# Attention feeding a two-layer PReLU network: three reorderings where one batch element's second layer hands over to the next one's first layer

## The chip, the core and the metric

One NeuronCore of a Trainium2 chip runs the whole program. The metric is the device time of one execution in microseconds (us); lower is better. The profile shows one execution with every instruction of TensorE (PE, its weight loads as PEld), VectorE (DVE), ScalarE (ACT), GpSimd (POOL) and the issue queue of SyncE (SP, its rows are SPq).

## The reference

Four batch elements, eight heads, 768 positions, head width 64. Attention is restricted by hashing: a query sees only keys whose six sign bits under a random projection agree with its own. Its output, as 3072 tokens of width 512, goes through two layers with a PReLU between them:

```python
scores = np.where(q_bucket == k_bucket, scale * q @ k.T, -1e9)
attn = softmax(scores)                       # per batch element and head
x = (attn @ v).transpose(0, 2, 1, 3).reshape(3072, 512)
h = x @ w_in                                 # 512 x 2048
g = np.maximum(h, 0) + alpha * np.minimum(h, 0)
out = g @ w_out                              # 2048 x 512
```

All tensors are float32.

## The kernel before

The program has two stages. Until about 313 us it runs the attention for all 16 pairs of heads and prepares the weights. After that it runs the two layers for each batch element b from 0 to 3, 768 tokens at a time, as a list `blocks`: for each b eight blocks `"1"` (first layer, `ff1`) and seven blocks `"2"` (second layer, `ff2`). A fallback program behind a flag never runs with these inputs.

**Seven products instead of eight.** Each layer splits both operands in halves both ways, and forms the product of the 2 x 2 blocks from seven block products with sums of blocks (the scheme of Strassen, in Winograd's form). `Product` holds the steps of one block: step 1, 2, 5, 6, 3, 7, 4 are groups of matmuls into the PSUM tiles a, b and c, each followed by copies on ScalarE or additions on VectorE. Step 22 is only VectorE work: additions of what steps 1 and 2 made. Step 4 is the last one; its matmuls go into a, and the addition after it (`finish("21", ...)`, the row L1243 `m<-m,z_4a` where the block is the second layer's last) completes the block and frees the PSUM slot.

**Sums ahead of the products.** x's halves for element b are `x_0`, `x_1`, `x_2`, `x_5`; `sum_x(b, n, DVE)` (L891) makes the four derived operands `x_3` to `x_6`, one for each n. `x_6`, of n = 3, is read only by step 4 of a first-layer block.

**The nested unit.** For b = 1, 2 and 3 two of the seven first-layer products are themselves formed by seven products, for four blocks at a time. `unit(b, u, before)` does that for blocks 4u to 4u + 3, by two `Inner` objects, `one` (operand `x_0`) and `two` (operand `x_3`), whose steps it interleaves with the last step of the block before it, `before.step(4)`. Matmul rows of `one` write na, nb, nc, those of `two` nd, ne, nf (L1084). Tiles a, c and d come from a pool of three PSUM slots (`two_banks`), which z_4a uses as well: nd takes the slot of z_4a.

The nested products need sums of their own. `sum_inner_x(b, o)` (L1062 to L1064) makes three tensors `xn` out of x_0 (o = 0) or x_3 (o = 1); the first reader of the latter is nf. `sum_inner(b, u, o)` (L1051) makes four nested sums of w_in, tile `wn` for o = 0 and `wp` for o = 1; it works for b = 1 alone, and after each sum GpSimd stores it to memory (`w_n_s`, L1052), from where b = 2 and 3 load it. The first reader of `wn`'s sums is nc, that of `wp`'s is nf.

**Order.** `do` keeps the instructions of an engine in the order in which the program makes them; `pinned` does so only under a condition, and what is not pinned is placed by a scheduler. Every engine works through its own list in order: an instruction that waits holds up all behind it on that engine. The order of calls around the handover is written by hand. In the block that ends a batch element (`"2"`, n == 6) it is: step 22, steps 5 (begun earlier), 6 and 3, `sum_inner(b + 1, 0, 0)`, step 7, `sum_inner_x(b + 1, 1)`, `sum_x(b + 1, 3, DVE)`; then `unit` begins.

**Output.** `turn_out` transposes a finished quarter of the output on VectorE (L1271) into a tile `o` and stores it by twelve DMAs (L1278), each of 32 partitions with rows of 256 bytes. The quarters are named by p: 2 and 3 are stored in the second layer, 5 and 4 both at the end of the next `unit`. All are issued by SyncE, but for four of the last batch element. SyncE also issues nearly all loads, among them each first-layer block's weights (`load_w`, L897, tile `wi`, three buffers, so that block n + 3's load waits until block n is done).

Of the kernel before, what the change touches and what calls it, by code (L numbers as in the profile page):

```python
# [407 lines left out]
def fast_path(  # L408
# [12 lines left out]
    nc = tc.nc  # L421
    P = 128
    B, H, S, D = q.shape
# [20 lines left out]
    PE, DVE, ACT, POOL = nc.tensor, nc.vector, nc.scalar, nc.gpsimd  # L444
# [253 lines left out]
    def two_banks(name):  # L698
        return psum.tile([P, 2, 512], F32, name=name, tag="sc", bufs=3)
# [172 lines left out]
    def pinned(when, ins):  # L872

        if when:
            do(ins)
# [10 lines left out]
    def sum_x(b, n, engine):  # L886

        to, a, c = ((3, 5, 0), (5, 2, 5), (4, 2, 3), (6, 4, 1))[n]
        if to != 5:
            x_m[b, to] = mid.tile([P, 2, CW], F32, name=f"x{b}_{to}", tag=f"x{to}", bufs=1)  # L890
        do(engine.tensor_tensor(x_m[b, to], x_m[b, a], x_m[b, c], op=ALU.subtract))  # L891
# [154 lines left out]
    def sum_inner(b, u, o):  # L1046

        if b != 1:
            return
        for m, x, op, y in ((3, 21, ALU.add, 2), (4, 3, ALU.subtract, 0), (5, 0, ALU.subtract, 21), (6, 1, ALU.subtract, 4)):  # L1050
            do(DVE.tensor_tensor(n_w[b, u, o, m], n_w[b, u, o, x], n_w[b, u, o, y], op=op))  # L1051
            nc.gpsimd.dma_start(w_n_s[u, o, :, m - 3].rearrange("p (t f) -> p t f", t=2), n_w[b, u, o, m])  # L1052

    def sum_inner_x(b, o):

        x = x_m[b, 3 * o]
        if o == 0:
            t = mid.tile([P, 4, HC], F32, name=f"xn{b}_0", tag="x", bufs=1)
        else:
            t = late[0].tile([P, 4, HC], F32, name=f"xn{b}_1", tag="gs5", bufs=1)  # L1060
        left, right = (x[:, :, c * HC : (c + 1) * HC] for c in range(2))
        do(DVE.tensor_tensor(t[:, :2], right, x[:, 0].rearrange("p (c w) -> p c w", c=2), op=ALU.subtract))  # L1062
        do(DVE.tensor_tensor(t[:, 2], right[:, 1], t[:, 0], op=ALU.subtract))
        do(DVE.tensor_tensor(t[:, 3], left[:, 1], t[:, 2], op=ALU.subtract))  # L1064
        n_x[b, o] = {0: left[:, 0], 1: left[:, 1], 2: right[:, 1], 3: t[:, 0], 4: t[:, 2], 5: t[:, 1], 6: t[:, 3]}
# [68 lines left out]
    def unit(b, u, before):  # L1134

        def bank(name, tag=None):
            name = f"n{name}{b}_{u}"
            return psum_bc[0].tile([P, 512], F32, name=name, tag=tag) if tag else two_banks(name)[:, 0]

        one = Inner(b, u, 0, bank("a"), bank("b", "b"), bank("c"))  # L1140
        one.step(1)
        one.step(5)
        before.step(4)
        one.step(2)
        one.step(6)
        if not u:
            sum_inner(b, 0, 1)
        two = Inner(b, u, 1, bank("d"), bank("e", "b"), bank("f", "c"))
        two.step(1)
        one.step(3)  # L1150
        two.step(5)
        one.step(7)
        two.step(2)
        two.step(6)
        one.step(4)
        two.step(3)
        now = ff1(b, 4 * u)
        now.step(1)
        two.step(7)
        now.step(2)  # L1160
        now.step(5)
        two.step(4)
        if u:
            sum_w2(b, 0, 3, 4, 6, 5)
        turn_out()
        return now

# [35 lines left out]
    def sides_g(b, n):  # L1203
        t = g_m[b, SIDES[ORDER[n]][1]]
        for m, kh, ch in ((0, 0, 0), (1, 1, 0), (2, 1, 1), (12, 0, 1)):
            g2[b, n, m] = t[:, kh * HK : (kh + 1) * HK, ch * HC : (ch + 1) * HC]

    def sum_w2(b, n, *ms):

        if n < 7:  # L1210
            for m in ms:
                x, op, y = {
                    3: (21, ALU.add, 2), 4: (3, ALU.subtract, 0), 5: (0, ALU.subtract, 21), 6: (1, ALU.subtract, 4),
                }[m]
                w2[b, n, m] = t = late[0].tile([P, HK, H2], F32, name=f"ws{b}_{n}_{m}", tag=f"ws{m}", bufs=1 + (m < 5))
                do(DVE.tensor_tensor(t, w2[b, n, x], w2[b, n, y], op=op))  # L1216
# [49 lines left out]
    def turn_out():  # L1266
        while to_turn:
            b, p, half, ch = to_turn.pop(0)
            o = late[0].tile([P, CW, 2], F32, name=f"o{b}_{p}", tag="o")
            for i in range(2):  # L1270
                do(DVE.transpose(o[:, :, i], m2[b, p][:, i]))  # L1271

            src = o.rearrange("p (c w d) i -> p c w (d i)", c=CH, d=32)
            for a in range(DM // 128):
                for c in range(CH):
                    cols = slice(half * DM // 2 + 64 * a, half * DM // 2 + 64 * a + 64)
                    queue = nc.gpsimd if (b, p) == (B - 1, 3) and c % 2 else nc.sync
                    pinned(b + 1 < B, queue.dma_start(  # L1278
                        out_v[b, ch * CH + c].rearrange("(w r) d -> r w d", r=32)[:, :, cols],
                        src[32 * a : 32 * a + 32, c],  # L1280
                    ))
# [187 lines left out]
    for j, (b, what, n) in enumerate(blocks):  # L1469
        n2 = n + 1 if what == "2" else 0 if n == NI - 1 else 7  # L1470
        if n2 == 0:
            sides_g(b, 0)
            if b == 0:
                sum_w2(b, 0, 3, 4)
        if not j:
            now.step(6)
        elif not (b and what == "1"):
            now.step(2)
        if j == 0:
            now.step(3)  # L1480
            now.step(7)
            now.step(2)
        now.step(22)
        if (b, what, n) == (1, "2", 1):
            largest()
        if what == "2" and b + 1 < B and 2 <= n < 6:
            if n == 3:
                sum_inner_x(b + 1, 0)
            else:
                sum_x(b + 1, {2: 0, 4: 1, 5: 2}[n], DVE)  # L1490
        if b and what == "1" and n == 1:
            load_inner(b, 1)
        if b and what == "1" and n in (2, 3):
            sum_inner(b, 1, n - 2)
        if 0 < n2 < 7:
            sides_g(b, n2)
            sum_w2(b, n2, 3, 4)
        if n2 < 7:
            sum_g2(b, n2, 3, 4)
        if j:  # L1500
            if not (b and what == "1"):
                now.step(5)
            now.step(6)
            now.step(3)
            if n2 or b == 0:
                sum_w2(b, n2, 6)
            if what == "2" and n == 6 and b + 1 < B:
                sum_inner(b + 1, 0, 0)
            if b and what == "1" and (n + 1) % 4:
                after = ff1(b, n + 1)  # L1510
                after.step(1)
            now.step(7)
            if n2 or b == 0:
                sum_w2(b, n2, 5)
            sum_g2(b, n2, 5)
        if (b, what, n) == (1, "2", 3):
            verdict()

        for n_out in [(), (0,), (1,), (2, 3), (4,), (5, 6), (7,)][j] if j < 7 else ():
            sum_out(n_out)  # L1520
        for n_out in [(1,), (2, 3), (4,), (5, 6), (7,)][j] if j < 5 else ():
            load_out(n_out)
        if what == "1":
            load_w(b * NI + n + 3)

            if b and n in (2, 5):
                load_w2(b, n // 4)
            if not b and n >= NI - 2:
                load_w2(b, n - NI + 2)
        else:  # L1530
            load_w2(b, n + 2)
            if b + 1 < B:
                if n == 5:
                    load_inner(b + 1, 0)
                if n == 0:
                    load_x(b + 1)
                if n == 6:
                    sum_inner_x(b + 1, 1)
                    sum_x(b + 1, 3, DVE)
        if j + 1 == len(blocks):  # L1540
            turn_last(0)
        elif what == "1" or n < 6:
            turn_out()
        before = now
        if j + 1 < len(blocks):
            b1, what1, n1 = blocks[j + 1]
            if b1 and what1 == "1" and n1 % 4 == 0:
                now = unit(b1, n1 // 4, before)
            elif b1 and what1 == "1":
                now = after  # L1550
                now.step(2)
                now.step(5)
                before.step(4)
            else:
                now = ff1(b1, n1) if what1 == "1" else ff2(b1, n1)
                now.step(1)
                before.step(4)
        else:
            before.step(4)
        if n2 < 7:  # L1560
            sum_g2(b, n2, 6)
# [29 lines left out]
```

## Time and profile before

| | us |
|---|---|
| median of 3 runs | 866.96 (865.55 to 867.17) |
| the profiled execution | 867.4 |
| its span, first to last instruction | 865.6 |
| attention stage | 0 to 313 |
| first layer b = 0 | 313 to 385 |
| handover to b = 1, 2, 3 (first matmul `na`) | 449.60, 585.65, 720.47 |

The profile's busy table gives, for each engine, its busy time, the share of the span and the instructions. A row of a timeline has start, duration, engine, line, operation, output <- inputs, shapes and the number of merged instructions; in square brackets stands how long the engine sat idle before it and what released it. Matmuls are pipelined and their ends are modelled, so the distance between the starts of two groups says more than a duration does. A row of waits says which group of instructions waited for which, for how long in total, how many times and for how long at most.

### The profile page before, as it was taken

The page shows a single profiled execution, that of the slowest core. Times are in us where ns is not written, and L with a number is a line of the kernel's source. Part 1 is how long each engine was busy: PE and PEld are TensorE (multiplying, and loading weights), DVE is VectorE, ACT ScalarE, POOL GpSimd, SP SyncE. Part 2 cuts the span into 40 slices and gives each one's busy share as a digit, 9 for nine tenths or more (in the row PEclk, how much of TensorE's full clock was granted, in tenths as well). Part 3 has the DMA queues.
Part 4 walks back from the last instruction along what each step waited for, and adds up shares of the span by engine and source line. Part 5 has one row for each costly group of instructions (what it writes and reads, how often), then busy time and mean ns, then how long its engine had stood idle before and what let it go on. Part 6 is the DMA issues. An engine that isn't in the chain of part 4 may idle for free.

```text
span 865.6 us, 15105 instructions
## 1 busy us (share of the span) xinstructions
PE 853.1 (99%) x5602; PEld 590.5 (68%) x5602; DVE 751.6 (87%) x1210; ACT 415.7 (48%) x778; POOL 123.8 (14%) x265
## 2 busy tenths in 40 slices
PE   9999999999999999999999999999999999999996
PEld 4444444444444445569997769997668998577996
DVE  6999999999999977899995979996769997668986
ACT  7777888878788833331115541114452114353111
POOL 1322423333334310210000100000000000000001
PEclk9999999999999999999999999999999999999999
DMA  8966879879697436776342935343845434650242
GB/s 198 184 141 131 199 178 244 167 202 246 131 249 209 146 126 237 247 283 225 116 137 69 348 135 169 121 148 82 310 150 177 141 109 122 215 219 5 98 153 72
DMA packets 180036, 147.97 MB, mean 171 GB/s; under 512 B 126977, under 2 KB 161969, under 8 KB 176369
## 3 DMA queue, kind: packets, MB, share of 16 engines
q1 hardware_dynamic: 166688, 118.92, 47.1%
q0 software_dynamic: 10256, 26.66, 10.0%
q10 hardware_dynamic: 3008, 1.33, 0.6%
q8 instruction: 46, 0.75, 0.4%
q14 instruction: 38, 0.30, 0.1%
HBM read 115.35 MB, written 30.41 MB: 168 GB/s over the span
## 4 chain that ended last, share of the span: by engine, by line


## 5 line engine op out<-in xcount | busy, mean ns | idle before, releaser
L790 ACT ACTIVATE pt<-sc 128x768 f32<-128x768 f32 x192 | 153.9, 813 | 3.0 <-PE sc L787 2.8
L787 PE MATMUL sc<-qT,kT 64*128 64x384 f32 x768 | 155.3, 482 | 0.0
L820 PE MATMUL av<-pt,vn 128*32 128x385 f32 (+1 forms) x1536 | 127.0, 485 | 0.0
L820 PEld LDWEIGHTS av<-pt,vn 128*32 128x32 f32 x1536 | 50.3, 109 | 73.8 <-issue 69.2
L787 PEld LDWEIGHTS sc<-qT,kT 64*128 64x128 f32 x768 | 68.5, 187 | 37.6 <-issue 37.3
L983 DVE TENSOR_TENSOR g<-g,g 128x384 f32<-128x384 f32 (+1 forms) x92 | 63.5, 711 | 1.6
L787 PE MATMUL sc<-qb,kb 64*128 64x384 bf16 x384 | 63.5, 323 | 0.7 <-DVE alpha L563 0.4
L979 DVE SCALAR_TENSOR_TENSOR g<-h,alpha 128x384 f32<-128x384 f32 x63 | 37.8, 612 | 21.3 <-ACT h L972 21.2
L1278 POOL DMA_DIRECT2D out_dram<-o x4 | 2.2, 560 | 363.5 <-DVE o L1271 363.5
L1224 DVE TENSOR_TENSOR gs<-g,gs 128x768 f32<-128x768 f32 x56 | 53.2, 951 | 1.0
L1224 DVE TENSOR_TENSOR gs<-g 128x768 f32<-128x768 f32 x56 | 53.2, 950 | 0.0
L1216 DVE TENSOR_TENSOR ws<-wl 128x512 f32<-128x512 f32 x56 | 38.4, 685 | 8.9 <-DMA wl<-w_out_s 7.7
L787 PEld LDWEIGHTS <-kb 64*128 64x128 bf16 x384 | 19.7, 94 | 34.7 <-issue 11.7
L607 ACT ACTIVATE wr<-raw 128x512 int32<-128x512 uint32 x32 | 22.1, 692 | 30.6 <-DVE wso L651 15.4
L798 DVE TENSOR_TENSOR accp<-pt,pt 128x1536 f32<-128x1536 f32 x16 | 28.1, 1756 | 7.1 <-ACT pt L790 7.1
L748 POOL DMA_DIRECT2D qb<-hr x60 | 30.0, 507 | 25.9 <-ACT hr L743 25.9
L803 DVE TENSOR_TENSOR accd<-accd,pt 128x1536 f32<-128x1536 f32 x16 | 28.1, 1758 | 1.7
L809 DVE TENSOR_TENSOR accd<-accd,accp 128x1536 f32<-128x1536 f32 x16 | 28.1, 1758 | 0.6
L806 DVE TENSOR_TENSOR accp<-accp,pt 128x1536 f32<-128x1536 f32 x16 | 28.0, 1753 | 0.0
L802 DVE TENSOR_TENSOR accd<-pt,pt 128x1536 f32<-128x1536 f32 x16 | 28.0, 1751 | 0.0
L1428 ACT ACTIVATE qT<-qT 128x768 f32<-128x768 f32 x15 | 12.7, 844 | 25.3 <-DMA kb<-hr 20.9
L1236 DVE TENSOR_TENSOR m<-m,m 128x768 f32<-128x768 f32 x24 | 22.7, 946 | 0.3
(448 smaller groups left out, 1862.1 us busy)
## 6 DMA issues: line engine op xcount, KB each, us to landing
wi<-w_in_s SPq DMA_DIRECT2D x32, 896.0 KB
wl<-w_out_s SPq DMA_DIRECT2D x16, 1024.0 KB
wl<-w_out_r SPq DMA_DIRECT2D x12, 1024.0 KB
raw<-in_moe_w_in_dram POOLq DMA_DIRECT2D x15, 512.0 KB, 4.7
raw<-in_moe_w_out_dram POOLq DMA_DIRECT2D x14, 512.0 KB, 4.7
w_in_s<-wsi SPq DMA_DIRECT2D x16, 448.0 KB
qn<-in_q_dram SPq DMA_DIRECT2D x64, 96.0 KB
vn<-in_v_dram SPq DMA_DIRECT2D x16, 384.0 KB
```

Of the source, the lines that this page charges most:

```text
L748: queue.dma_start(bits[name, pi][D * s : D * s + 2 * NB, half * CW : (half + 1) * CW], raw[c : c + 2 * NB],)
L787: do(PE.matmul(sc[:, s, :CW], what["k", pi][r, ks], what["q", pi][r, qs], start=first, stop=not first,))
L790: do(ACT.activation(pts[kc][:, g, :, :CW], sc[:, :, :CW], AF.Exp, scale=SCALE / DOWN))
L798: do(DVE.tensor_tensor(accp[pi], p(0), p(1), op=ALU.add))
L802: do(DVE.tensor_tensor(accd[pi], p(3), p(4), op=ALU.add))
L803: do(DVE.tensor_tensor(accd[pi], accd[pi], p(5), op=ALU.add))
L809: do(DVE.tensor_tensor(accd[pi], accd[pi], accp[pi], op=ALU.add))
L820: do(PE.matmul(av[pi][D * s + t : D * s + t + 32, g, :w], nat["v", pi][:, s, kc * D + t : kc * D + t + 32], pts[kc][:, g, s, :w], start=(k ...
L979: do(DVE.scalar_tensor_tensor(new_g(b, m)[:, i], h, al, h, op0=ALU.mult, op1=ALU.max))
L983: do(DVE.tensor_tensor(new_g(b, to)[:, at], g_m[b, x][:, at], g_m[b, y][:, at], op=ALU.subtract))
L1216: do(DVE.tensor_tensor(t, w2[b, n, x], w2[b, n, y], op=op))
L1224: do(DVE.tensor_tensor(t, g2[b, n, x], g2[b, n, y], op=ALU.subtract))
```

## The change

Three things are moved, and no computation is added or left out.

1. `sum_inner_x(b + 1, 1)` and `sum_x(b + 1, 3, DVE)`, which stood at the end of the block before, go into `unit` for u = 0: the first behind `one.step(2)`, so behind the last addition of `before.step(4)`; the second behind `sum_inner(b, 0, 1)`.
2. `sum_inner(b + 1, 0, 0)`, the nested w_in sums of `wn`, goes from behind step 3 to before step 22, so before the block's additions on VectorE.
3. In `turn_out`, for b < 3, the stores of chunks c = 1 and 2 of the quarters p = 5 and 4 are issued by GpSimd, 16 of 24. They are not pinned in the program's order.

```diff
         before.step(4)
         one.step(2)
+        if not u:
+            sum_inner_x(b, 1)
         one.step(6)
         if not u:
             sum_inner(b, 0, 1)
+            sum_x(b, 3, DVE)
...
-                    queue = nc.gpsimd if (b, p) == (B - 1, 3) and c % 2 else nc.sync
-                    pinned(b + 1 < B, queue.dma_start(
+                    queue = nc.gpsimd if ((b, p) == (B - 1, 3) and c % 2 or b + 1 < B and c and p in (5, 4)) else nc.sync
+                    pinned(b + 1 < B and queue is nc.sync, queue.dma_start(
...
+        if what == "2" and n == 6 and b + 1 < B:
+            sum_inner(b + 1, 0, 0)
         now.step(22)
...
-            if what == "2" and n == 6 and b + 1 < B:
-                sum_inner(b + 1, 0, 0)
...
-                if n == 6:
-                    sum_inner_x(b + 1, 1)
-                    sum_x(b + 1, 3, DVE)
```

On TensorE and ScalarE the order of instructions stays as it was. On VectorE the three x sums and `x_6` follow the last addition and the addition of nb, and at the handover to b = 1 the order becomes: last addition, nb addition, three x sums, four `wp` sums, `x_6`. On SyncE's queue the order of two loads changes at each handover: `wl_0`, the second layer's first weights, comes ahead of one of the loads of `wi`.

## The prediction

> **What bounds the kernel now.** I read the busy table first, then the waits of TensorE, then the timelines of TensorE, VectorE and SyncE around the three places where the second layer of one batch element meets the nested unit of the next. I call them handover A (to b = 1, at 449.6 us), B (b = 2, 585.65) and C (b = 3, 720.47).
>
> ```profile
> PE 853.1 (99%) x5602; PEld 590.5 (68%) x5602; DVE 751.6 (87%) x1210; ACT 415.7 (48%) x778; POOL 123.8 (14%) x265
> ```
>
> TensorE has hardly an idle moment, so a change can gain only what TensorE waits for. GpSimd (POOL) is nearly free.
>
> ```profile
> PE nd L1084 <- DVE m L1243: 1.6, 3, 1.0
> ...
> PE f_3b L921 <- DMA wi<-w_in_s: 0.9, 1, 0.9
> PE nc L1084 <- DVE wn L1051: 0.8, 1, 0.8
> ```
>
> Columns: us in total, times, longest. Of TensorE's few waits these three are the large ones after the start, and all lie at the handovers. First A, TensorE and then VectorE:
>
> ```profile
> 449.60 0.81 PE L1084 MATMUL na<-x,wn 128*128 128x192 f32 x4
> 451.22 0.92 PE L1084 MATMUL nc<-xn,wn 128*128 128x192 f32 x4 [0.80 <-DVE wn L1051]
> 451.97 1.46 PE L921 MATMUL z_4a<-gs,wl 128*128 128x192 f32 x8
> ...
> 453.92 0.81 PE L1084 MATMUL na<-xn,wn 128*128 128x192 f32 x4
> 455.00 0.92 PE L1084 MATMUL nd<-x,wq 128*128 128x192 f32 x4 [0.27 <-DVE m L1243]
> 455.75 0.81 PE L1084 MATMUL nc<-x,wn 128*128 128x192 f32 x4
> ```
>
> ```profile
> 450.75 1.54 DVE L1051 TENSOR_TENSOR wn<-wn 128x256 f32<-128x256 f32 x4
> ...
> 453.73 0.95 DVE L891 TENSOR_TENSOR x<-x,x 128x768 f32<-128x768 f32 x1
> 454.60 0.34 DVE L1243 TENSOR_TENSOR m<-m,z_4a 128x192 f32<-128x192 f32 x1
> 454.87 0.55 DVE L1119 TENSOR_TENSOR n<-n_0p,nb 128x384 f32<-128x384 f32 x1
> ```
>
> Undisturbed groups of four start 0.65 apart. na to nc takes 1.62 and nc to z_4a 0.75: the wait for the nested w_in sums costs 0.97 + 0.10 = 1.07 (the idle figure, 0.80, leaves out the exposed weight load and the slower first group). na to nd takes 1.08, nd to nc 0.75: 0.43 + 0.10 = 0.53. VectorE was late: at 453.4 z_4a had ended, but its last addition (L1243), whose end frees the PSUM slot that nd takes, stood behind four sums of x. The same at B and C, and C's late load on TensorE and on SyncE's queue (SPq):
>
> ```profile
> 588.90 0.81 PE L1084 MATMUL na<-xn,wn 128*128 128x192 f32 x4
> 590.71 0.92 PE L1084 MATMUL nd<-x,wq 128*128 128x192 f32 x4 [1.00 <-DVE m L1243]
> 591.47 0.81 PE L1084 MATMUL nc<-x,wn 128*128 128x192 f32 x4
> ```
>
> ```profile
> 724.94 0.92 PE L1084 MATMUL nd<-x,wq 128*128 128x192 f32 x4 [0.32 <-DVE m L1243]
> ```
>
> ```profile
> 748.31 1.45 PE L921 MATMUL f_2a<-x,wi 128*128 128x384 f32 x4
> 750.69 1.53 PE L921 MATMUL f_3b<-x,wi 128*128 128x384 f32 x4 [0.93 <-DMA wi<-w_in_s]
> 752.05 1.45 PE L921 MATMUL f_2a<-x,wi 128*128 128x384 f32 x4
> ```
>
> ```profile
> 733.14 12.67 SPq L1278 DMA_DIRECT2D out_dram<-o  x24
> 745.90 0.38 SPq L897 DMA_DIRECT2D wi<-w_in_s  x1
> ```
>
> B's nd loses 1.16 + 0.11 = 1.27, C's 0.49 + 0.10 = 0.59 (na at 723.80, nc at 725.69). C's f_3b came 2.38 after f_2a where the pitch is 1.29, and 1.36 before the next: 1.09 + 0.07 = 1.16. Its weights were issued at 745.90, behind 24 output stores.
>
> **What the Trainium skill says.** "Perfetto Trace Analysis", section "Identifying the Most-Contended Engine": matmul busy time says little of roofline; look for the gaps of the busiest engine and the semaphore behind each. Here the gaps are small and named. "DMA: Bandwidth & Descriptors", section "Issuing engines are not separate DMA queues": a second issuing engine saves only sequencer time. Here that is the point: 24 stores hold SP 12.67 us. "SBUF — State Buffer", section "SBUF: two separate sides": GpSimd builds its descriptors through a port pair that some VectorE operations lock. The trace shows no such collision: while GpSimd issued four stores from 451.46 (0.54 each), VectorE's x sums took 0.55 and 0.95, as in C where GpSimd was idle.
>
> **The change part by part.** No instruction is added or removed; TensorE and ScalarE keep their order, VectorE's changes at the handovers, and 48 store issues (16 for each) go from SP to GpSimd.
>
> *Late sums of x (A, B, C).* Three sums (0.58 + 0.40 + 0.27 to the next start) and x_6 (0.87), 2.12 us of VectorE, go behind the last addition and the nb addition. VectorE now waits for z_4a, then for nb, with the sums queued behind. In B: z_4a ends at 588.41, the addition runs 588.5 to 588.86; nd is due at 589.55: no wait. nb ends at 589.06, its addition 589.16 to 589.70, the first x sum to 590.25; nf, its first reader, is due at 590.85. C has the same distances. x_6 is not read until f_0's last step, about 8 us later; the nc addition slips under 1 us, and its reader, the seed of f_0b, comes 3 us after. Gain 0.53 + 1.27 + 0.59 = 2.39.
>
> *w_in's nested sums earlier (A alone).* Four sums, 1.46 us, start at 449.03 behind the second layer's last g sum instead of at 450.75. The first, all that nc needs, ends at 449.45; nc is due at 450.25. na used the tile from 449.6 unhindered, so it had landed by then: at worst 0.4 later, still in time. Their four stores on GpSimd go along (2.16 us, read back a batch element later). The five additions behind slip 1.46: the first frees p1 at 450.84 (ScalarE overwrites it from 451.1), z_4b's frees its bank at 451.3 (nb wants it at 452.2), the fifth starts at 452.21, and the last addition runs 452.5 to 452.8, nd being due at 453.5. Gain 1.07.
>
> *A new wait in A.* The second block's nested w_in sums (L1051, wp) stay on VectorE before x_6, but now come behind the x sums. From nb's end, 453.1: addition, three x sums, first wp sum 454.82 to 455.23. nf is due at 454.80 and starts at about 455.3: 0.49 + 0.10 = **0.59 lost**. The other wp sums (to 456.3) are due only three groups later. This wait isn't in the trace of before, so it is bounded: 0.3 if VectorE takes up each operation a little sooner than I assume, 1.0 if the first nested sums must wait 0.4 for their tile. I take the worked-out value.
>
> *Stores on GpSimd.* Of each 24 stores of o_5 and o_4, 16 leave SP: 16/24 of 12.67 is 8.4 us in C (7.5 in A, 7.6 in B). SP then reaches f_3's load at 737.5, where its buffer, f_0's, is free only at about 739.4; with the 4.7 us that it took (745.90 to 750.6) it lands at 744, f_3b being due at 749.6. Gain 1.16 in C; A and B made it without a wait. Behind that waiting load SP holds the next unit's weights, which come 5 to 6 us earlier than now anyway; At each handover w_out's first tile also overtakes one w_in load (f_4's at A, f_5's at B and C). That load waits for a buffer still in use anyway (f_1's or f_2's) and has over 10 us to its use: nothing. GpSimd pays 16 x 0.56 (its last stores at 852.38 took 2.21 for four) = 9 us per handover, behind which at A only stores for later wait: nothing. The end of the program is untouched, since the last batch element keeps its stores.
>
> **Sum.** 2.39 + 1.07 - 0.59 + 1.16 = **4.03**. The profiled execution took 867.4 (span 865.6), 0.44 above the median 866.96. 867.4 - 4.0 = 863.4 for it, **863.0** for the median. With nf's bounds 862.6 to 863.3.
>
> **Rivals.**
> - *The new wait grows*: nf also waits in B and C, where my margin is 0.6, by some 0.6 each, and A's wait reaches 1.0. For it: VectorE is late there by up to 1 us. Against: it idles 1.27 right after. Gain 2.4, time 864.5.
> - *The load stays late*: the stores on GpSimd slow the same DMA engines, or the order holds it. Gain 2.9, time 864.1. Against: they move the same bytes, and the DMA share is 0.42 from 720 to 792.
> - *Given back*: in the second layer VectorE is busy 62 of 64.5 us; a TensorE that comes sooner finds it late (as z_2c did, 0.37 at 398.8). Gain under 1.7, time 866. Against: VectorE idles several times per f block before it, and catches up.
> - *Slower*: each GpSimd issue holds VectorE through the shared ports. From 598 to 617 in B VectorE idles 1.14 + 0.52 + 1.37 + 0.99 + 0.52 + 1.37 = 5.9 us. A hold of 0.56 is 9.0 us, 3.1 too many, three times: 867 + 9.3 - 4.0 = 872. It decides from a hold of about 0.45 (16 x 0.45 - 5.9 = 1.3, the gain of one handover). Against: the undisturbed sums at 451.46.
>
> **How the numbers follow.** Forecast 0.70, growing wait 0.10, late load 0.08, given back 0.06, slower 0.06. A measurement of this kernel can tell about 0.2%, 1.7 us, from no change. Faster 0.88, same 0.06, slower 0.06. The likeliest is 863.0; the range 861.8 to 865.2 takes in the spread of the runs (1.6 us), nf's bounds and the first two rivals.
>
> **What would show it.** Right: the waits nd on m, nc on wn and f_3b on wi are gone, a wait of nf on wp stands once with 0.5, the SP row before f_3's load counts 8 stores, GpSimd has 48 more. Wrong: nf waiting three times, VectorE's sums longer under GpSimd's issues, or TensorE waiting in the second layer.

## The result, and the profile after

The changed kernel takes **864.13 us** (median of 17 runs, 862.94 to 866.87) against 867.55 for the kernel before on the same chips (17 runs, 865.55 to 868.53): a ratio of **0.9967 (95% interval 0.9959 to 0.9974)**, so a gain of about 2.9 us (2.3 to 3.6). The ratio is that of the means, 864.43 and 867.32; the medians lie 3.4 apart. The forecast was 863.0, from a gain of 4.0: the direction held and the time fell into the range, but the gain came out more than a quarter smaller than forecast.

The profiled execution took 865.96, span 863.8, which is 1.8 above the kernel's own median: its waits are not all typical, as will be seen. In what follows lines behind L1143 stand three higher than before: L1243 is now L1246, L1245 is L1248, L1216 is L1219, L1278 is L1281.

The busy table of the changed kernel:

```profile
PE 851.8 (99%) x5602; PEld 591.1 (68%) x5602; DVE 751.6 (87%) x1210; ACT 415.9 (48%) x778; POOL 150.1 (17%) x313
```

GpSimd has 48 instructions more (265 to 313) and 26.3 us more of work. VectorE's 751.6 us are the same as before to the tenth. TensorE's waits (us in total, times, longest):

```profile
PE z_2c L921 <- DVE m L1248: 0.8, 1, 0.8
PE z_3a L921 <- DMA wl<-w_out_s: 0.6, 1, 0.6
...
PE nf L1084 <- DVE wp L1051: 0.4, 1, 0.4
...
PE z_4c L921 <- DVE m L1248: 0.3, 1, 0.3
PE z_7c L921 <- DVE m L1248: 0.2, 1, 0.2
```

The three rows of nd, f_3b and nc are gone, and the one new row that was announced is there, nf on wp, once. But there are rows of the second layer (z_2c, z_3a, z_4c, z_7c) which the page of before had not, or had smaller. The largest of them is no effect of the change:

```profile
398.75 1.57 PE L921 MATMUL z_2c<-gs,ws 128*128 128x192 f32 x8 [0.78 <-DVE m L1248]
```

It stands in the second layer of b = 0, some 50 us before the first of the moved instructions (448.90 below), at the place where the forecast had seen 0.37 before. Handover A, TensorE and then VectorE:

```profile
449.55 0.81 PE L1084 MATMUL na<-x,wn 128*128 128x192 f32 x4
450.20 0.81 PE L1084 MATMUL nc<-xn,wn 128*128 128x192 f32 x4
...
453.45 0.81 PE L1084 MATMUL nd<-x,wq 128*128 128x192 f32 x4
454.10 0.81 PE L1084 MATMUL nc<-x,wn 128*128 128x192 f32 x4
455.27 0.92 PE L1084 MATMUL nf<-xn,wp 128*128 128x192 f32 x4 [0.36 <-DVE wp L1051]
456.03 0.81 PE L1084 MATMUL na<-xn,wn 128*128 128x192 f32 x4
```

```profile
448.90 1.55 DVE L1051 TENSOR_TENSOR wn<-wn 128x256 f32<-128x256 f32 x4
...
452.36 0.35 DVE L1246 TENSOR_TENSOR m<-m,z_4a 128x192 f32<-128x192 f32 x1
...
454.80 0.42 DVE L1051 TENSOR_TENSOR wp<-wq 128x256 f32<-128x256 f32 x1
```

nc follows na by 0.65, the undisturbed distance, and nd its predecessor likewise. nf starts 1.17 after nc instead of 0.65, and the next group 0.76 after nf: 0.52 + 0.11 = 0.63 lost. VectorE's rows show why each holds: the `wn` sums run before the additions, the last addition ends at 452.71, 0.74 before nd, and the first `wp` sum ends at 455.22, just ahead of nf.

At C the load of f_3's weights, on SyncE's queue and then on TensorE:

```profile
730.96 3.70 SPq L1281 DMA_DIRECT2D out_dram<-o  x8
737.30 0.34 SPq L897 DMA_DIRECT2D wi<-w_in_s  x1
```

```profile
746.14 1.45 PE L921 MATMUL f_2a<-x,wi 128*128 128x384 f32 x4
747.43 1.45 PE L921 MATMUL f_3b<-x,wi 128*128 128x384 f32 x4
```

Eight stores instead of 24 stand ahead of the load, it is issued 8.6 us earlier on the clock (745.90 to 737.30), and f_3b comes 1.29 after f_2a: no wait.

So every view shows the change at work as described. By stages, from the start of na to the start of f_0b (f_0b is a group of the first-layer block f_0, behind the unit's first part):

| us | before, three profiles | after | gain on their mean | forecast |
|---|---|---|---|---|
| A | 11.35, 11.32, 11.40 | 10.38 | 0.98 | 1.01 |
| B | 11.02, 11.02, 11.02 | 9.75 | 1.27 | 1.27 |
| C | 10.42, 10.29, 9.85 | 9.75 | 0.44 | 0.59 |
| f_0b to z_1a at b = 3 | 61.22, 61.35, 60.32 | 60.06 | 0.90 | 1.16 |

The gains on the mean sum to 3.6. The first of the three profiles is the one that the forecast used; the other two (below) are of the same kernel. Two terms were priced from an execution that had more of the wait than others have. Against the measured 2.9, some 0.7 must be lost elsewhere.

### The profile page after: what moved, and what is told of

It reads as the page before. It is cut to its first block, busy times and chain, and to the rows that moved or that the text cites. A ratio compares the mean times of both kernels' runs of the same rounds, so it can differ in the third digit from the quotient of the medians.

```text
span 863.8 us, 15130 instructions
## 1 busy us (share of the span) xinstructions
PE 851.8 (99%) x5602; PEld 591.1 (68%) x5602; DVE 751.6 (87%) x1210; ACT 415.9 (48%) x778; POOL 150.1 (17%) x313
## 4 chain that ended last, share of the span: by engine, by line
## 5 line engine op out<-in xcount | busy, mean ns | idle before, releaser
L1281 POOL DMA_DIRECT2D out_dram<-o x52 | 28.3, 552 | 349.6 <-DVE o L1274 348.8
L1219 DVE TENSOR_TENSOR ws<-wl 128x512 f32<-128x512 f32 x56 | 38.4, 685 | 11.3 <-DMA wl<-w_out_s 9.7
```

The costliest lines, as they stand in the source:

```text
L1281: pinned(b + 1 < B and queue is nc.sync, queue.dma_start(out_v[b, ch * CH + c].rearrange("(w r) d -> r w d", r=32)[:, :, cols], src[32 * a ...
```

## The experiments

**Part 1 alone: x's late sums.** Against the kernel before:

```diff
         one.step(2)
+        if not u:
+            sum_inner_x(b, 1)
         one.step(6)
         if not u:
             sum_inner(b, 0, 1)
+            sum_x(b, 3, DVE)
...
-                if n == 6:
-                    sum_inner_x(b + 1, 1)
-                    sum_x(b + 1, 3, DVE)
```

> Only the late sums of x (first part of the change). My theory, a sum of separate waits: the three waits of nd go (0.53 + 1.27 + 0.59 = 2.39), the new wait of nf on wp at A costs 0.59, the waits of nc on wn (1.07) and of f_3b on its load (1.16) stay: about 1.8 us faster than before, ratio 0.998. Rival 'it was the freed queue': the stores made the gain, so no change here. Rival 'given back': VectorE's lateness in the second layer eats it, under 0.8 us.

Measured: 865.83, ratio 0.9983 (0.9974 to 0.9992), a gain of 1.5 where 1.8 was expected. In the list of TensorE's waits nd is gone at all three handovers, and there remain:

```profile
PE f_3b L921 <- DMA wi<-w_in_s: 1.3, 2, 1.1
...
PE nc L1084 <- DVE wn L1051: 0.8, 1, 0.8
PE nf L1084 <- DVE wp L1051: 0.4, 1, 0.4
```

nf's wait comes with part 1 and needs neither of the others.

**Part 2 alone: w_in's nested sums earlier.** Against the kernel before:

```diff
+        if what == "2" and n == 6 and b + 1 < B:
+            sum_inner(b + 1, 0, 0)
         now.step(22)
...
-            if what == "2" and n == 6 and b + 1 < B:
-                sum_inner(b + 1, 0, 0)
```

> Only w_in's nested sums earlier (second part). My theory: nc no longer waits, but VectorE's chain up to the last addition is no shorter, since the four sums of x still stand before it, so nd waits until the same moment as before: nd's wait at A grows from 0.53 to about 1.6 and the gain is 0 (within 0.3 us). Rival 'each part brings its own share': 1.07 us faster, ratio 0.9988, nd's wait unchanged.

Measured: 867.06, ratio 0.9997 (0.9988 to 1.0006). The wait of nc is gone, and yet nothing is gained, since nd pays it back:

```profile
PE nd L1084 <- DVE m L1243: 2.3, 2, 1.3
```

The longest wait, 1.3, is at A, where it was 0.27. VectorE's queue has the same work ahead of the last addition in either order, so as long as x's sums stand ahead of it, a TensorE that passes nc sooner only meets nd sooner.

**Part 3 alone: the stores.** Against the kernel before:

```diff
-                    queue = nc.gpsimd if (b, p) == (B - 1, 3) and c % 2 else nc.sync
-                    pinned(b + 1 < B, queue.dma_start(
+                    queue = nc.gpsimd if ((b, p) == (B - 1, 3) and c % 2 or b + 1 < B and c and p in (5, 4)) else nc.sync
+                    pinned(b + 1 < B and queue is nc.sync, queue.dma_start(
```

> Only the stores shared with GpSimd (third part). My theory: f_3b's wait at C goes and nothing else, 1.2 us faster, ratio 0.9987; all waits of nd and nc as before; VectorE's operations under the GpSimd issues keep their durations. Rival 'it was the freed queue': most of the gain is here, 2.5 to 3.5 us. Rival 'GpSimd holds VectorE': no gain or a loss.

Measured: 866.77, ratio 1.0003 (0.9995 to 1.0012). f_3b's wait was gone from the profile, and the time had not moved: the expectation was missed, and so was a term of the forecast. That the rival "no gain or a loss" came true doesn't make its reason right (GpSimd holding VectorE); see the part on the rivals.

**The `wp` sums ahead of the nb addition.** Against the changed kernel, to take away nf's wait:

```diff
         before.step(4)
+        if not u:
+            sum_inner(b, 0, 1)
         one.step(2)
         if not u:
             sum_inner_x(b, 1)
         one.step(6)
         if not u:
-            sum_inner(b, 0, 1)
             sum_x(b, 3, DVE)
```

> The changed kernel, with the four wp sums moved ahead of the nb addition and the x sums at the handover to b = 1. My theory: the new wait of nf at A (0.4 idle, 0.5 to 0.6 in the distance of starts) shrinks to 0.1 or goes; 0.5 us faster than the changed kernel, ratio to before about 0.996. Rival: nf then waits as long for the x sums, which now stand behind the wp sums: no change to the changed kernel.

Measured: 864.26, ratio 0.9968 (0.9958 to 0.9979), as the changed kernel. nf has two operands, and now waits for the other, `xn`:

```profile
PE nf L1084 <- DVE xn L1062: 0.3, 1, 0.3
```

**The kernel before, profiled twice more.** No edit. The question was whether the second layer's waits come from the change, and how steady f_3b's wait is.

> The kernel before, profiled a second time. Four other kernels show at b = 1, in the second layer, a wait of z_7c and of z_4c on VectorE (0.22 and 0.29 idle, 0.39 + 0.45 in the distance of starts) after a load of w_out's tile that took 6.0 to 6.4 us; the first profile of before had 5.45 us and only 0.23. 'It is chance of an execution': here they stand too, and f_3b's wait at C is another than 1.1. 'The change's kernels pay for it': the load takes 5.4 to 5.5 us again and the waits are missing.

> The kernel before, profiled a third time, with the same question: how long does the wait of f_3b at C last (1.1 in the first profile; my sum rests on it), and do z_7c and z_4c wait at b = 1.

Measured: executions of 867.68 and 867.28. TensorE's waits in the first of them:

```profile
PE f_3b L921 <- DMA wi<-w_in_s: 1.1, 1, 1.1
...
PE z_4c L921 <- DVE m L1245: 0.3, 1, 0.3
PE z_7c L921 <- DVE m L1245: 0.2, 1, 0.2
```

z_4c and z_7c wait in both, by the same 0.3 and 0.2 as in the changed kernel. They were missing from the first profile of before, and they are no price of the change. What varies is a 1 MB load of w_out at b = 1: in the first profile VectorE took up the tile 5.45 us after the load's issue, in the two new ones after 6.25 and 6.47, in the changed kernel after 6.24. f_3b's lateness (its distance from f_2a beyond the usual 1.29) was 1.22 in the first new profile and 0.18 in the second.

**Parts 1 and 2, all stores on SyncE.** The edits of part 1 and part 2 together, and the line of part 3 undone:

```diff
-                    queue = nc.gpsimd if ((b, p) == (B - 1, 3) and c % 2 or b + 1 < B and c and p in (5, 4)) else nc.sync
+                    queue = nc.gpsimd if (b, p) == (B - 1, 3) and c % 2 else nc.sync
```

> The late x sums and the early w_in sums together, all stores on SP. My theory: the two parts together bring the 1.07 that w_in's sums alone did not, 2.39 + 1.07 - 0.59 = 2.9 us faster than before, ratio 0.9967, as the whole change; f_3b waits at C and by 0.2 to 0.4 at A. Rival 'the stores are what makes TensorE's gain last': f_3b gives back what the handover gained, under 2.0 us.

Measured: 864.11, ratio 0.996 (0.9946 to 0.9974). Within the noise this is the whole gain, without part 3. Part 2, which gave nothing alone, gives its term once part 1 has cleared the way. From the start of na to that of f_0b, A takes 11.40 us with part 1 alone (nd's wait goes, nf's comes), 11.35 with part 2 alone (nc's wait goes, nd's grows) and 10.38 with both; before it was 11.36 in the mean. f_3b was late by 0.19 at C and did not wait at A, less than expected.

**x's sums, then the `wp` sums, both ahead of the nb addition.** Against the changed kernel:

```diff
         before.step(4)
+        if not u:
+            sum_inner_x(b, 1)
+            sum_inner(b, 0, 1)
         one.step(2)
-        if not u:
-            sum_inner_x(b, 1)
         one.step(6)
         if not u:
-            sum_inner(b, 0, 1)
             sum_x(b, 3, DVE)
```

> The changed kernel, but at the handover to b = 1 VectorE makes the x sums, then the wp sums, and only then the nb addition. My theory: z_4a's end plus last addition, three x sums and the first wp sum is 0.3 us ahead of nf, so no wait of nf is left; ne waits for the nb addition by 0.1 at most. 0.5 us faster than the changed kernel, ratio to before 0.996. Rival: the wait moves on to ne, whose bank the later nb addition frees: no change.

Measured: 864.15, ratio 0.9967 (0.9955 to 0.9979). nf no longer waits. The nb addition is now last, and what depends on it is late instead, through ScalarE, so it is the rival that came:

```profile
PE ne L1084 <- ACT ne L1108: 0.3, 1, 0.3
```

**Part 3 again**, the same edit as before, to settle its size.

> Only the stores shared with GpSimd, measured once more, since the first comparison (1.0003) left out the 1.16 us of my sum. The six profiles with all stores on SP show f_3b's wait at C as 1.16, 1.22, 1.22, 0.46, 0.19 and 0.18 in the distance of starts, 0.74 in the mean. Theory 'the term was one execution's, the mean counts': 0.3 to 0.7 us faster than before, ratio 0.9992 to 0.9997, no wait of f_3b. Rival 'GpSimd's issues cost as much elsewhere': ratio 1.000 or above, and an added wait in the profile outside C.

Measured: 868.18, ratio 1.0011 (1.0001 to 1.0021): no gain, if anything a small loss. Of TensorE's waits, and of VectorE's timeline, in this kernel's profile:

```profile
PE nc L1084 <- DVE wn L1051: 1.6, 1, 1.6
```

```profile
441.73 0.69 DVE L1216 TENSOR_TENSOR ws<-wl 128x512 f32<-128x512 f32 x1 [1.01 <-DMA wl<-w_out_r]
```

f_3b does not wait, but nc waits 0.8 longer than before. VectorE had stood 1.01 for a load of w_out, taken up 6.5 us after its issue at 435.27, and carried the delay to A. In the first profile of before the same step found its tile there without a wait, 5.4 us after issue. This is one execution and does not show that the stores slow the loads: in the first profile of part 3 alone nc waited 0.9.

**Small VectorE work moved away.** `largest` and `verdict` (13 small VectorE operations, 1.8 us, which decide on the fallback) stand in the second layer of b = 1, where z_7c and z_4c wait. Against the changed kernel:

```diff
-        if (b, what, n) == (1, "2", 1):
+        if (b, what, n) == (2, "1", 5):
             largest()
...
-            if (b, what, n) == (1, "2", 3):
+            if (b, what, n) == (2, "1", 6):
```

> The changed kernel, with the thirteen small VectorE operations of largest() and verdict() (1.8 us, which decide whether the fallback runs) moved from the second layer of b = 1 to the first layer of b = 2, blocks 5 and 6. Theory: z_7c and z_4c wait at b = 1 because these operations come on top of a VectorE that a late load has already put behind; the second layers of b = 2 and 3, without them, show no such wait. So both waits go, 0.8 us faster than the changed kernel, ratio to before 0.9958. Rival 'the load alone does it': the waits stay, no change.

Measured: 864.8, ratio 0.9975 (0.9967 to 0.9983): no gain; by the ratios it is some 0.7 behind the changed kernel, but the two intervals overlap. z_7c and z_4c wait no more, but at b = 2, where the second layer starts, there are new waits:

```profile
659.24 1.57 PE L921 MATMUL z_1c<-gs,ws 128*128 128x192 f32 x8 [0.27 <-DVE f_7u L975]
...
669.12 1.57 PE L921 MATMUL z_2c<-gs,ws 128*128 128x192 f32 x8 [0.52 <-DVE m L1248]
```

In the profiles, from z_1a to the next na, the second layer of b = 1 takes 63.97 instead of the changed kernel's 64.98, and that of b = 2 takes 65.01 instead of 63.75: what one gains the other loses. The first layer of b = 2 had looked free, since before the change VectorE was busy there for 50.05 of 70.40 us; its end has no slack, for z_1c waits for the last additions of f_7.

**One sum of each kind first.** Against the changed kernel, with `sum_inner_x` and `sum_inner` split into parts, so that what nf needs comes first and what ne needs is not pushed back:

```diff
         before.step(4)
+        if not u:
+            sum_inner_x(b, 1, 0)
         one.step(2)
         if not u:
-            sum_inner_x(b, 1)
+            sum_inner(b, 0, 1, slice(0, 1))
+            sum_inner_x(b, 1, 1)
         one.step(6)
         if not u:
-            sum_inner(b, 0, 1)
+            sum_inner(b, 0, 1, slice(1, 4))
             sum_x(b, 3, DVE)
```

> The changed kernel, with the order on VectorE behind the last addition: first x sum, nb addition, first wp sum, then the other sums. Theory: in the kernel with wp first nf waited on the x sums (0.33), in the one with nb last ne waited on nb's bank (0.40); with only the two sums that nf needs ahead, and the nb addition between them, neither waits. 0.5 us faster than the changed kernel, ratio to before about 0.996. Rival: some other sum is then late (nd's or the second nf's), a wait of 0.3 or more stays at A.

Measured: 864.23, ratio 0.997 (0.9958 to 0.9982). In the profile A has no wait left (nf starts 0.65 after nc): from na to f_0b it takes 9.75 us instead of 10.38, as B and C do. The profiled execution, 862.95, is as fast as the fastest of the changed kernel (862.94). But the time did not follow for certain. The mean of the runs is 863.97 against 864.43 for the changed kernel; of these 0.46 only 0.17 lies inside the span (862.05 against 862.22), the rest is time outside it, and the intervals overlap almost wholly: not settled.

**Both of the last two.** The edits of "one sum of each kind first" and of "small VectorE work moved away" in one kernel, both as above.

> Both of these together, as a version to beat the changed kernel: 0.5 + 0.8 us faster than it, ratio to before about 0.995. Rival: TensorE, earlier by so much, finds the load of the second layer's tile late and gives half of it back.

Measured: 864.75, ratio 0.9976 (0.9968 to 0.9984), with the same new waits at b = 2. The second edit's price stands, and no kernel here is measurably better than the changed one.

## Why the forecast was right, and where it was off

*Late sums of x (forecast 2.39).* The mechanism is shown: nd's waits go in the kernel with this part alone and in every kernel that has it. B's 1.27 was exact: the stage takes 11.02 in every profile without this part and 9.75 in every one with it. C's 0.59 was mis-sized: the stage was 0.67, 0.54 and 0.10 longer in the three profiles of before than after the change, 0.44 in the mean, and the forecast used the first.

*w_in's nested sums earlier (1.07).* Right, and conditional. The forecast summed it with the part before without saying that it is worth nothing without it. The runs show it: 0.9997 alone, and the full gain together.

*The new wait of nf (−0.59).* It cost 0.63, at A alone. Two reorderings moved it to `xn` and to ne. Only the split order removed it from the profile, and made A shorter by 0.63 there.

*Stores on GpSimd (1.16).* **This is the step that failed**, twice. First the size: f_3b's lateness, its distance from f_2a beyond 1.29, in the six profiles of kernels that keep all these stores on SyncE was 1.09, 1.22, 1.22, 0.47, 0.19 and 0.18, mean 0.73. (The forecast's 1.16 counts 0.07 for the group behind it as well.) The forecast took one of the large ones for the whole. Second, the forecast said that the end of the program is untouched. Its last matmuls in the first profile of before, and in the changed kernel:

```profile
858.51 0.44 PE L1292 MATMUL tz<-ident,m 128*128 128x128 f32 x2
```

```profile
856.08 0.44 PE L1295 MATMUL tz<-ident,m 128*128 128x128 f32 x2
```

From there it is 7.1 us to the end of the span before (865.6) and 7.7 after (863.8), with the same work. Over all profiles, counted from the second of these two matmuls, it is 6.9 to 7.3 with the stores on SyncE (six profiles, mean 7.1) and 7.2 to 7.6 with the shared stores (eight profiles, mean 7.4). The time outside the span is recorded for every run. It is 1.80 in the mean of 138 runs of kernels with the stores on SyncE (1.74 to 1.92), and 2.19 in 89 runs of five of the seven kernels with the shared stores (2.11 to 2.30). Together that is 0.3 + 0.4 = 0.7 us, as much as the shared stores save in the mean. In the kernel with part 3 alone the balance is nil or a small loss (1.0003 and 1.0011; inside the span its mean was 0.6 shorter the first time and 0.4 longer the second, outside it 0.4 longer both times), and the whole gain is there without it (0.996).

Why the end takes longer was not found. The part outside the span is no fixed price of the shared stores, since the other two kernels that have them show less of it: "small VectorE work moved away" and "one sum of each kind first", 1.89 in the mean of 23 runs. Inside the span the traces show one place. SyncE's eight closing semaphore steps, first before, then after the change (count, shortest, median and longest in ns, first and last start):

```profile
L403 SPq EVENT_SEMAPHORE  x8: 17/17/17, 860.8 to 863.9; - x8
```

```profile
L403 SPq EVENT_SEMAPHORE  x8: 17/17/17, 861.6 to 862.1; - x8
```

In all six profiles with the stores on SyncE three of the eight come 2.1 to 2.3 us after the last matmul and the other five behind a pause; in all eight with shared stores the pause comes first, and all eight follow it. From the end of that pause to the end of the span it is 2.04 us in the former and 2.23 in the latter, which is 0.2 of the 0.3. What moved the pause stays open.

So the measured 2.9 is the forecast's 2.39 + 1.07 − 0.59 = 2.87 with a stores term near zero; or, by stages on the means, 3.6 − 0.7 = 2.9. That both come out so close is in part luck, for the measured interval is 1.3 wide.

*The rivals.* "The new wait grows" did not occur: nf waits once. "The load stays late" gave 864.1, as measured, but by a cause that is refuted: f_3b waits in none of the eight profiles with shared stores. "Given back" seemed to be borne out by the four rows of the second layer. But z_2c's 0.8 comes before anything was moved, and z_7c and z_4c are in before as well. z_3a's wait of 0.6 followed a load that VectorE took up 7.1 us after its issue (818.90 to 826.00). It stood in the kernel with all stores on SyncE too (0.9), but in none of the other five that have parts 1 and 2, so it is no regular price of an earlier TensorE; whether an earlier TensorE makes it more likely is not shown. "Slower", GpSimd holding VectorE, is refuted: VectorE's busy time is equal to the tenth with 26.3 us more issuing on GpSimd. GpSimd was not held up either: its 52 stores took 0.549 to 0.574 us each to issue. So the port collision that the Trainium skill's page "SBUF — State Buffer", section "SBUF: two separate sides", warns of does not show for these operations. (The evidence that the forecast had for it was thinner than it said: GpSimd's four issues from 451.46 had ended at 453.62, before the x sum of 0.95 began at 453.73, so only the three shorter ones overlapped.) What the page "DMA: Bandwidth & Descriptors" says in "Issuing engines are not separate DMA queues" held: a second issuer saved sequencer time (24 stores in 12.67 us became 8 in 3.70).

*The range* took in the miss, because it reached to the case in which the stores bring nothing.

## What to carry to other kernels

When a wait is removed from an engine whose queue runs in order, look for the next instruction that is late behind it: an edit can be worth nothing alone and all of its price with another one, and work moved out of a wait needs a place with slack, which the share of busy time doesn't show. Price a wait for a transfer from several profiled executions, since one may show six times what another does. A step that was "free" because its engine was idle may come with a longer end of the program, as here: compare the tail of the span and the time outside it as well.

## What was not expected of the hardware

- Sharing 48 small stores with GpSimd came with up to 0.7 us more at the program's end, 0.3 in the span and, in five of seven kernels, 0.4 outside it, though the last stores of the program were the same.
- Where VectorE waited for a 1 MB load of w_out, the load had taken from 5.45 to 7.3 us from issue to use (5.45, 6.25 and 6.47 at the same place of b = 1 in three executions of one kernel), and late ones reached TensorE as waits of 0.2 to 0.9, at once or some groups later. Much of the kernel's spread (865.55 to 868.53 before) is of the size of such waits; that it consists of them was not shown. In the six profiles of kernels whose order is the same up to A, the second layer of b = 0 took from 63.7 to 65.5 us up to na.
- GpSimd issued a store of 32 partitions with rows of 256 bytes in 0.55 us, as steadily as 0.549 to 0.574, SyncE in 0.43 in the median (0.315 to 1.592).
